# Another order of the seven products, and other places for their results, in a fused convolution and feed-forward kernel

## The chip, the cores and the metric

The kernel runs on one core of a Trainium2 chip. The metric is device time in microseconds (us), the median of several executions of one program; lower is better.

## The reference

`x` is 2048 rows of 1024. It is normalised by rows; `xn` goes into two branches whose results are added to `x`.

```python
xn = _layernorm(x)                         # x = A_q, 2048 x 1024
# A: gated convolution
k_shift = short causal convolution of k with shift_k (4 taps, per channel)
kv  = k_shift * v
y   = long causal convolution of kv with ssm_k (2048 taps, per channel) + kv * ssm_D
A   = xn * y
# B: feed-forward
h   = silu(xn @ w1)                        # w1: 1024 x 3584
B   = h @ w2                               # w2: 3584 x 1024
out = x + A + B
```

## The kernel before

**Products.** All matmuls take float16 operands, each split into a high and a low part, so one product of two blocks is three matmuls per chunk of 128 (lines L946 to L948 for `xn @ w1`, called GEMM1; L1074 to L1076 for `h @ w2`, called GEMM2).

**Seven in place of eight.** Most of GEMM1 and a part of GEMM2 multiply 2 x 2 blocks by seven products of sums and differences, named P1 to P7 (`PRODUCTS`, L50). `x` is held as seven sums (A11, A12, A22, S1 to S4), the weights likewise (B11, B21, B22, T1 to T4). One such group of products is a *unit*: in GEMM1 a pair of weight column blocks `i` for one half `sp` of the rows (12 units in the first half, 14 in the second, `UNITS`), in GEMM2 a quarter of the row tiles of one half (8 units, `tiles2`, `units2`). A product in a unit is twelve matmuls of 512 columns.

**Banks.** The products of a unit share PSUM banks of the ring `ff` (four banks). Bank `one` takes P1, then P2 on top. Bank `two` begins as a copy of P1 made by ScalarE (`ff<-ff` in the trace); P6 is added to it; ScalarE copies the sum out (called `u` in GEMM1, `a` in GEMM2); P5 is added; ScalarE copies it again (`d`); P3 is added. Bank `c` takes P7; VectorE forms c + d; P4 is added; VectorE forms c + u. Before, the order on TensorE is P1, then P7, P6, P2, P5, the next unit's P1, P3, P4. `units` and `units2` issue the products, `evacuate` and `evacuate2` empty the banks. A `Token` in `seen` stands for "copied out, the bank may be added to", one in `made` for "product done".

**Places in SBUF.** `places` are eight places of 1 MB: they hold the seven sums of `x`, later the converted blocks of `w2` (`W2PLACE` and `FPLACE` say which place, in the order in which the products leave them). The sums of the second half of the rows are brought by transposing loads on SyncE's queue (`load_x`, line L342), each as soon as its place is left by the first half. Place 4 holds A21 at first and then the *quads*: the results of the pairs of blocks 8 to 11 (`PAIRS`), which GEMM2 will use in seven products too (`quad`, `room`).

**Results** go through `hfs`, three tiles of two halves each (`hf` in the trace; `vs_r` and `ws_r` are the same object), and a second such object `hts` with two tiles (`ht`). A half is chosen by this rule, where `two` are the tiles of which both halves are free:

```python
k, h = min(self.free(), key=lambda q: (q[0] in two, self.age[q[0]]))
```

In `evacuate2` results leave as accumulating stores to `out`, issued by GpSimd (`G`, line L346). The very last block is instead loaded, added to and stored by SyncE's queue (`L`, line L336), to end sooner.

**GEMM2's plain part** takes the rows in two passes over the columns (`h`), in five chunks `c` of `w2`. `TOGETHER` says which row tiles are done at once: the first two in the first pass and the last three in the second share a chunk before the next is taken.

**The convolution** is a chain of transforms in eight groups of 128 channels beside all this: matmuls at L1520 to L1522 (forward) and L1711 to L1713 (back), much VectorE work (line L349, `spec` and `tmp`). `spare` lets it use a bank of `ff` in GEMM2's plain part if more than one is free.

**Order.** All instructions are put in an order at build time by a planner (`Order.run`): each generator is a stream; the planner takes the stream whose next instruction could begin first by its own estimates, less a small bias. A place or bank counts as free in the planner as soon as the last instruction that uses it has been put in order. On the chip each engine runs its instructions in that order and waits at semaphores.

Of the kernel before, what the change touches and what calls it, by code (L numbers as in the profile page):

```python
# [11 lines left out]
F32 = mybir.dt.float32  # L12
# [8 lines left out]
P = 128  # L21
# [4 lines left out]
NT = S // P  # L26
# [274 lines left out]
def h3_ffn_kernel(ctx, tc, x, kp, vs, fs, shift, dskip, w1, w2, cfwd, cinv, out):  # L301
# [559 lines left out]
    def room():  # L861

        for sp in range(2):
            yield flag["room", sp]
            yield places[4].ready
            t, tok = places[4].tile([P, 2, 2 * W], F32)
            parts.open(t, 2)
            yield flag["quads", sp]
            tok.set()
# [36 lines left out]
            add(blocks(i, b, hf, tok, (made,)), EB)  # L906
        return hf, made

    def evacuate(i, b, one, c, made, seen):
# [29 lines left out]
        add(silu(i, low, low, None, done), EB)  # L939

    def steps(o, w, xf, first, last, more=False):

# [39 lines left out]
    def units():  # L982

        todo = [(i, sp) for sp in range(2) for i in UNITS[sp]]
        yield ff.ready
        one = ff.tile([P, 4, P])
        yield from product("P1", *todo[0], one[0], True)
        for n, (i, sp) in enumerate(todo):
            if sp == 1:
                flag["unit", n - len(UNITS[0])].set()  # L990
                flag["room", 1].set()
            if i in PAIRS:
                add(quad(i, sp), 0.1)
            made, seen = defaultdict(Token), defaultdict(Token)
            yield ff.ready
            c = ff.tile([P, 4, P])
            add(evacuate(i, 2 * sp, one, c, made, seen), EB)
            yield from product("P7", i, sp, c[0], True)
            yield seen["P1"]
            two = seen["bank"][0]  # L1000
            yield from product("P6", i, sp, two)
            made["P6"].set()
            yield from product("P2", i, sp, one[0])
            made["P2"].set()
            yield seen["P6"]
            yield from product("P5", i, sp, two)
            made["P5"].set()
            if n + 1 < len(todo):
                yield ff.ready
                one = ff.tile([P, 4, P])  # L1010
# [5 lines left out]
            yield from product("P4", i, sp, c[0])  # L1016
# [14 lines left out]
    def feed_forward():  # L1031
# [13 lines left out]
        for h in range(2):  # L1045
            for ts in TOGETHER[h]:
# [34 lines left out]
    def uses2():  # L1081

        yield 0, "P1"
        for u in range(len(tiles2)):
            for n in ("P7", "P6", "P2", "P5"):
                yield u, n
            if u + 1 < len(tiles2):
                yield u + 1, "P1"
            yield u, "P3"
            yield u, "P4"  # L1090

    def units2():
# [8 lines left out]
            if u == len(tiles2) - 1:  # L1101
                wtok.set()

        yield ff.ready
        one = ff.tile([P, W])
        yield from product2("P1", 0, one[0], True)
        for u in range(len(tiles2)):
            made, seen = defaultdict(Token), defaultdict(Token)
            yield ff.ready
            c = ff.tile([P, W])  # L1110
            add(evacuate2(u, one, c, made, seen), EB)
            yield from product2("P7", u, c[0], True)
# [4 lines left out]
            yield from product2("P2", u, one[0])  # L1117
            made["P2"].set()
            yield seen["P6"]
            yield from product2("P5", u, two)  # L1120
            made["P5"].set()
            if u + 1 < len(tiles2):
                yield ff.ready
                one = ff.tile([P, W])
                yield from product2("P1", u + 1, one[0], True)
# [4 lines left out]
            yield from product2("P4", u, c[0])  # L1130
            made["P4"].set()

    def at(u, r, h):
# [2 lines left out]
        t = 4 * (2 * sp + r) + q  # L1136
        return orr[t // T2, t % T2, :, h * W:(h + 1) * W]

    def evacuate2(u, one, c, made, seen):
# [28 lines left out]
        seen["P7"].set()  # L1168
        yield G(at(u, 1, 1), d)
# [684 lines left out]
```

## Time and profile before

| what | us |
|---|---|
| median of 3 runs | 1257.39 (1256.72 to 1257.83) |
| the profiled execution | 1258.14 |
| its span, first to last instruction | 1256.4 |
| TensorE busy | 1232.6 (98%) |
| VectorE busy | 1117.9 (89%) |
| ScalarE busy | 790.5 (63%) |
| GpSimd busy | 83.5 (7%) |
| mean granted TensorE clock | 0.994 |

In the profile PE is TensorE, DVE VectorE, ACT ScalarE, POOL GpSimd, SP SyncE (SPq: what its queue issues). A row of the timeline has the start from the span's begin, the duration, engine and line, the operation with the tiles it writes and reads, the shapes, and in brackets the idle time before it and what ended that. A helper's line stands for all its calls: L349 two-operand VectorE operations, L352 the same with a scalar, L360 all ScalarE activations.

### The profile page before, as it was taken

To read this page: it belongs to the slowest core of one execution; us is meant where nothing else is said; L and a number is where in the kernel's file an instruction comes from. 1 tells how busy PE (TensorE), PEld (TensorE's weight loads), DVE (VectorE), ACT (ScalarE), POOL (GpSimd) and SP (SyncE) were. 2 spreads that over 40 slices of the span, in tenths; PEclk is the share of its full clock that TensorE was granted. 3 is DMA by queue.
4 is the path that set the end of the run, shared out by engine and by line. 5 is a ranking of instruction groups with operands and counts; after the bars stand their busy time and mean duration, and the time that the engine had idled before them with its cause. 6 is when DMAs were issued, how large, how long until landed. Compare 5 with 4: busy or idle time off the path is not lost. (4 is left out here: it accounts for less than half of the span.)

```text
span 1256.4 us, 17146 instructions
## 1 busy us (share of the span) xinstructions
PE 1232.6 (98%) x6034; PEld 597.5 (48%) x6034; DVE 1117.9 (89%) x1359; ACT 790.5 (63%) x1431; POOL 83.5 (7%) x93
## 2 busy tenths in 40 slices
PE   7999999999999999999999999999999999999996
PEld 6554444444444544444444544544544544454452
DVE  7999987997999789998999899799989889988970
ACT  7868888886588878568654643744653545563351
POOL 0000000000000000000000000000120030123132
PEclk8999999999999999999999999999999999999999
DMA  9276989989799899769984655688595497969765
GB/s 367 82 262 239 315 288 303 300 240 227 232 336 270 242 309 313 207 191 297 311 278 125 206 179 132 185 269 231 107 257 153 106 225 217 243 137 161 164 121 80
DMA packets 272662, 279.83 MB, mean 223 GB/s; under 512 B 73792, under 2 KB 192576, under 8 KB 271296
## 3 DMA queue, kind: packets, MB, share of 16 engines
q1 hardware_dynamic: 256848, 262.22, 67.9%
q0 software_dynamic: 15728, 16.52, 9.9%
q8 instruction: 47, 0.77, 0.3%
q14 instruction: 39, 0.32, 0.1%
HBM read 175.66 MB, written 88.34 MB: 210 GB/s over the span
## 5 line engine op out<-in xcount | busy, mean ns | idle before, releaser
L1074 PE MATMUL ff<-x,wo 128*128 128x512 f16 x864 | 327.9, 380 | 3.4 <-ACT hf L360 3.4
L1076 PE MATMUL ff<-x,wo 128*128 128x512 f16 x864 | 328.1, 380 | 0.0
L1075 PE MATMUL ff<-x,wo 128*128 128x512 f16 x864 | 327.9, 380 | 0.1
L946 PE MATMUL ff<-x,wo 128*128 128x512 f16 (+1 forms) x808 | 304.5, 377 | 6.2 <-ACT hf L360 3.0
L948 PE MATMUL ff<-x,wo 128*128 128x512 f16 (+1 forms) x808 | 304.8, 377 | 1.0 <-DVE wo L352 1.0
L947 PE MATMUL ff<-x,wo 128*128 128x512 f16 (+1 forms) x808 | 304.8, 377 | 0.0
L349 DVE TENSOR_TENSOR spec<-spec 128x512 f32<-128x512 f32 (+2 forms) x256 | 261.8, 1053 | 2.0
L1075 PEld LDWEIGHTS <-wo 128*128 128x128 f16 x864 | 84.6, 98 | 104.0 <-issue 4.7
L1076 PEld LDWEIGHTS <-wo 128*128 128x128 f16 x864 | 84.6, 98 | 102.6 <-issue 1.0
L1074 PEld LDWEIGHTS <-wo 128*128 128x128 f16 x864 | 85.5, 99 | 100.1 <-issue 0.6
L948 PEld LDWEIGHTS <-wo 128*128 128x128 f16 x808 | 79.6, 98 | 94.3 <-DVE wo L352 1.5
L947 PEld LDWEIGHTS <-wo 128*128 128x128 f16 x808 | 79.5, 98 | 93.8 <-issue 5.8
L946 PEld LDWEIGHTS <-wo 128*128 128x128 f16 x808 | 81.0, 100 | 90.2 <-ACT wo L360 1.7
L349 DVE TENSOR_TENSOR tmp<-spec 128x2048 f32<-128x2048 f32 (+1 forms) x48 | 92.7, 1933 | 0.9
L352 DVE SCALAR_TENSOR_TENSOR ht<-hf,wsc,ht 128x1024 f16<-128x1024 f32 (+1 forms) x56 | 67.4, 1203 | 7.5 <-ACT ht L360 7.2
L360 ACT ACTIVATE spec<-ps 128x512 f32<-128x512 f32 x92 | 53.2, 592 | 28.7 <-PE ps L1522 28.0
L352 DVE SCALAR_TENSOR_TENSOR wo<-raw,wsc,wo 128x512 f16<-128x512 f32 (+1 forms) x56 | 56.4, 1012 | 11.9 <-ACT wo L360 11.9
L346 POOL DMA_DIRECT2D out<-hf x47 | 45.8, 981 | 303.9 <-ACT hf L360 254.4
L360 ACT ACTIVATE hf<-ff,invc 128x512 f32<-128x512 f32 x32 | 21.9, 684 | 65.7 <-PE ff L1076 47.6
L360 ACT ACTIVATE ht<-hf,wsc 128x1024 f16<-128x1024 f32 (+1 forms) x56 | 60.8, 1085 | 3.4 <-DVE hf L349 2.1
L360 ACT ACTIVATE spec<-spec 128x1024 bf16<-128x1024 f32 x32 | 33.7, 1054 | 46.1 <-DVE spec L349 46.0
L349 DVE TENSOR_TENSOR spec<-tmp 128x512 f32<-128x512 f32 (+1 forms) x80 | 61.3, 792 | 0.7
(188 smaller groups left out, 1779.3 us busy)
## 6 DMA issues: line engine op xcount, KB each, us to landing
wo<-hs SPq DMA_DIRECT2D x160, 256.0 KB, 3.2
hs<-ht SPq DMA_DIRECT2D x80, 256.0 KB, 4.8
raw<-in_w SPq DMA_DIRECT2D x28, 512.0 KB, 5.9
wraw<-in_w SPq DMA_DIRECT2D x24, 512.0 KB, 5.4
w2n<-in_w SPq DMA_DIRECT2D x24, 512.0 KB, 6.1
out<-hf POOLq DMA_DIRECT2D x47, 256.0 KB, 4.5
kin<-in_kp SPq DMA_DIRECT2D x16, 704.0 KB, 5.1
xt<-in_x SPq DMA_DIRECT2D x16, 512.0 KB, 7.3
```

What stands on the lines that cost most here:

```text
L346: return Op("POOL", 1.1, 3.0, lambda: nc.gpsimd.dma_start(o, i, accum_op=ADD), [i], [o], m, 2.3 * n)
L349: return V(lambda: nc.vector.tensor_tensor(o, a, b, op=op), o, [a, b], **k)
L352: return V(lambda: nc.vector.scalar_tensor_tensor(o, a, s, b, op0=op0, op1=op1), o, [a, b] + ([] if isinstance(s, float) else [s]), **k)
L360: nc.scalar.activation(o, i, func, scale=scale, **kw)
L946: nc.tensor.matmul(o, w[:, 0, k], xf[:, :, k, 0], start=first and k == 0, stop=False, **kw)
L947: nc.tensor.matmul(o, w[:, 0, k], xf[:, :, k, 1], start=False, stop=False, **kw)
L948: nc.tensor.matmul(o, w[:, 1, k], xf[:, :, k, 0], start=False, stop=last and k == KH - 1, **kw)
L1074: nc.tensor.matmul(po, hx[:, n, 0, :], wc[:, n, 0, :], start=first and n == 0, stop=False, **kw)
L1075: nc.tensor.matmul(po, hx[:, n, 0, :], wc[:, n, 1, :], start=False, stop=False, **kw)
L1076: nc.tensor.matmul(po, hx[:, n, 1, :], wc[:, n, 0, :], start=False, stop=last and n == 3, **kw)
```

## The change

From the second unit on, in each of the two `units` functions, the order becomes P6, P7, P5, P2, next P1, P3, P4; the first unit keeps the old order. The emptying of a unit is started right after its P1 instead of after the unit before. The second half's S2 is loaded first, into place 4 (where the first half's quads were), and the second half's quads go to S2's old place 6; the other sums are loaded in the new order of use; `W2PLACE` and `FPLACE` follow. In GEMM2's first pass three row tiles share the chunks at the beginning instead of two. In the last unit the results of P1 with P2 and of P3, and the block that is loaded from `out`, may take a half of `hts` if none of `hfs` is free.

```diff
-W2PLACE = [(2, 7, 6, 3, 4), (0, 1, 5, 2, 7)]
-FPLACE = (6, 3, 4, 0, 1, 5, 2, 7)
+W2PLACE = [(2, 4, 7, 0, 3), (1, 5, 6, 2, 4)]
+FPLACE = (7, 0, 3, 1, 5, 6, 2, 4)
...
         for sp in range(2):
             yield flag["room", sp]
-            yield places[4].ready
-            t, tok = places[4].tile([P, 2, 2 * W], F32)
+            r = places[(4, XPLACE["S2"])[sp]]
+            yield r.ready
+            t, tok = r.tile([P, 2, 2 * W], F32)
...
-        yield made["P2"]
-        up, both = yield from places_of(i, b)
-        add(silu(i, up[:, 0], *one, both), EB)
+
+        def first():
+            up, both = quads_up[i, b] = yield from places_of(i, b)
+            add(silu(i, up[:, 0], *one, both), EB)
+        if early:
+            yield made["P2"]
+            yield from first()
         yield ws_r.ready
         d, dt = ws_r.tile([P, 4, P])
         yield made["P5"]
         yield a_act(d, two, AF.Copy)
         seen["P5"].set()
+        c = seen["c"]
+        if not early:
+            yield made["P2"]
+            yield from first()
+        up, both = quads_up.pop((i, b))
...
+        def start(n):
+            i, sp = todo[n]
+            yield ff.ready
+            one = ff.tile([P, 4, P])
+            yield from product("P1", i, sp, one[0], True)
+            made, seen = defaultdict(Token), defaultdict(Token)
+            add(evacuate(i, 2 * sp, one, made, seen, n == 0), EB)
+            return one, made, seen
...
+            if n == 0:
+                yield from seventh()
             yield seen["P1"]
             two = seen["bank"][0]
             yield from product("P6", i, sp, two)
             made["P6"].set()
-            yield from product("P2", i, sp, one[0])
-            made["P2"].set()
+            yield from second() if n == 0 else seventh()
             yield seen["P6"]
             yield from product("P5", i, sp, two)
             made["P5"].set()
+            if n > 0:
+                yield from second()
             if n + 1 < len(todo):
-                yield ff.ready
-                one = ff.tile([P, 4, P])
-                yield from product("P1", *todo[n + 1], one[0], True)
+                following = yield from start(n + 1)
...
-        for name in [p[0] for p in PRODUCTS.values()]:
-            r = places[XPLACE[name]]
+        for name in ("S2", "A11", "S3", "S1", "A12", "S4", "A22"):
+            r = places[4 if name == "S2" else XPLACE[name]]
...
-    TOGETHER = ([range(2)] + [(t,) for t in range(2, NT)],
+    TOGETHER = ([range(3)] + [(t,) for t in range(3, NT)],
...
-            for n in ("P7", "P6", "P2", "P5"):
+            for n in ("P7", "P6", "P2", "P5") if u == 0 else ("P6", "P7", "P5", "P2"):
...
         def copied(src, tok, to):
-            yield hfs.ready
-            o, otok = hfs.tile([P, W])
+            yield lambda: hfs.ready() or last and hts.ready()
+            o, otok = (hfs if hfs.ready() else hts).tile([P, W])
...
-        yield made["P2"]
-        add(copied(*one, at(u, 0, 0)), EB)
+        if u == 0:
+            yield made["P2"]
+            add(copied(*one, at(u, 0, 0)), EB)
         yield ws_r.ready
         d, dt = ws_r.tile([P, W])
         yield made["P5"]
         yield a_act(d, two, AF.Copy, invc2[:, 0:1])
         seen["P5"].set()
+        c = seen["c"]
         yield v_stt(d, c[0], invc2[:, 0:1], d, MUL, ADD)
         seen["P7"].set()
+        if u > 0:
+            yield made["P2"]
+            add(copied(*one, at(u, 0, 0)), EB)
         yield G(at(u, 1, 1), d)
         dt.set()
         if last:
             yield flag["conv out"]
-            yield hfs.ready
-            o, otok = hfs.tile([P, W])
+            yield lambda: hfs.ready() or hts.ready()
+            o, otok = (hfs if hfs.ready() else hts).tile([P, W])
```

`units2` is changed as `units` is, with its own `start`, `seventh` and `second`.

More of the change, by code (lines that the diff above doesn't have):

```diff
@@ L907, in places_of, with evacuate @@
         return hf, made
-    def evacuate(i, b, one, c, made, seen):
+    def evacuate(i, b, one, made, seen, early):
         yield ff.ready
@@ L939, in evacuate @@
         add(silu(i, low, low, None, done), EB)
+    quads_up = {}
     def steps(o, w, xf, first, last, more=False):
@@ L984, in units @@
         todo = [(i, sp) for sp in range(2) for i in UNITS[sp]]
-        yield ff.ready
-        one = ff.tile([P, 4, P])
-        yield from product("P1", *todo[0], one[0], True)
+        def start(n):
[6 more added lines that the diff above has]
+            return one, made, seen
+        following = yield from start(0)
         for n, (i, sp) in enumerate(todo):
@@ L993, in units, with seventh, second @@
                 add(quad(i, sp), 0.1)
[L994 to L998, printed above, removed]
+            one, made, seen = following
+            def seventh():
+                yield ff.ready
+                seen["c"] = c = ff.tile([P, 4, P])
+                yield from product("P7", i, sp, c[0], True)
+            def second():
+                yield from product("P2", i, sp, one[0])
+                made["P2"].set()
+            if n == 0:
+                yield from seventh()
             yield seen["P1"]
@@ L1015, in units @@
             yield seen["P7"]
-            yield from product("P4", i, sp, c[0])
+            yield from product("P4", i, sp, seen["c"][0])
             made["P4"].set()
@@ L1102, in product2, with start, seventh, second @@
                 wtok.set()
-        yield ff.ready
-        one = ff.tile([P, W])
-        yield from product2("P1", 0, one[0], True)
-        for u in range(len(tiles2)):
[L1108 to L1112, printed above, removed]
+        def start(u):
+            yield ff.ready
+            one = ff.tile([P, W])
+            yield from product2("P1", u, one[0], True)
+            made, seen = defaultdict(Token), defaultdict(Token)
+            add(evacuate2(u, one, made, seen), EB)
+            return one, made, seen
+        following = yield from start(0)
+        for u in range(len(tiles2)):
+            one, made, seen = following
+            def seventh():
+                yield ff.ready
+                seen["c"] = c = ff.tile([P, W])
+                yield from product2("P7", u, c[0], True)
+            def second():
+                yield from product2("P2", u, one[0])
+                made["P2"].set()
+            if u == 0:
+                yield from seventh()
             yield seen["P1"]
@@ L1116, in units2 @@
             made["P6"].set()
-            yield from product2("P2", u, one[0])
-            made["P2"].set()
+            yield from second() if u == 0 else seventh()
             yield seen["P6"]
@@ L1121, in units2 @@
             made["P5"].set()
+            if u > 0:
+                yield from second()
             if u + 1 < len(tiles2):
-                yield ff.ready
-                one = ff.tile([P, W])
-                yield from product2("P1", u + 1, one[0], True)
+                following = yield from start(u + 1)
             yield seen["P5"]
@@ L1129, in units2 @@
             yield seen["P7"]
-            yield from product2("P4", u, c[0])
+            yield from product2("P4", u, seen["c"][0])
             made["P4"].set()
```

6 lines of the change are left out of this document (3 added, 3 removed).

## The prediction

> **What bounds the kernel now.** I read the page first: how busy each engine is.
>
> ```profile
> PE 1232.6 (98%) x6034; PEld 597.5 (48%) x6034; DVE 1117.9 (89%) x1359; ACT 790.5 (63%) x1431; POOL 83.5 (7%) x93
> ```
>
> TensorE works in 1232.6 of 1256.4 us, and the change takes no matmul away. All that can be won is idle time, the clock that idle time costs, and what follows the last matmul. So the second view is the table of stretches (columns: stretch, length, busy time of PE, PEld, DVE, ACT, POOL, granted clock, DMA share, GB/s).
>
> ```profile
> 320.00:330.00 10.00, 8.24 (x39) 3.63 (x38) 9.96 (x9) 6.66 (x9) 0.76 (x1) 1.00 0.37 125
> 584.00:598.00 14.00, 11.04 (x44) 4.64 (x43) 11.85 (x13) 11.37 (x20) 0.00 (x0) 0.88 1.09 360
> 598.00:1077.00 479.00, 478.41 (x2325) 227.46 (x2323) 445.66 (x478) 247.26 (x505) 33.92 (x35) 1.00 0.71 199
> 1231.00:1257.00 26.00, 14.91 (x61) 6.09 (x59) 2.19 (x3) 2.75 (x4) 4.53 (x6) 0.87 0.48 76
> ```
>
> Three places lose time: 1.76 us in the first, 2.96 in the second with a clock of 0.88, and 11.1 in the last. The 479 us of plain GEMM2 lose 0.6. Third, the timeline of those places. The last unit of GEMM1, on PE and then on ACT:
>
> ```profile
> 584.66 0.38 PE L948 MATMUL ff<-x,wo 128*128 128x512 f16 x1
> 588.00 0.40 PE L946 MATMUL ff<-x,wo 128*128 128x512 f16 x1 [2.96 <-ACT hf L360]
> 588.22 0.61 PE L947 MATMUL ff<-x,wo 128*128 128x512 f16 x1
> ...
> 591.61 0.40 PE L1520 MATMUL ps<-hi,cfw 128*128 128x512 f16 x1
> ```
>
> ```profile
> 583.97 1.15 ACT L360 ACTIVATE x<-w2n,tau 128x1024 f16<-128x1024 f32 x1 [1.19 <-DMA w2n<-in_w]
> ...
> 587.37 0.58 ACT L360 ACTIVATE hf<-ff 128x512 f32<-128x512 f32 x1
> ```
>
> P5 ends at 585.04 (584.66 + 0.38); P3 adds into the same bank and may start only when ACT has copied it, and that copy, behind other work of ACT's, ends at 587.95. This last unit has no next P1 to put between them. The first unit of the second half waits for DVE instead:
>
> ```profile
> 318.72 4.61 DVE L349 TENSOR_TENSOR spec<-spec 128x2048 f32<-128x2048 f32 x2
> ...
> 325.63 0.69 DVE L349 TENSOR_TENSOR hf<-ff,hf 128x512 f32<-128x512 f32 x1
> ```
>
> ```profile
> 321.64 0.38 PE L948 MATMUL ff<-x,wo 128*128 128x512 f16 x1
> ...
> 324.23 0.38 PE L948 MATMUL ff<-x,wo 128*128 128x512 f16 x1
> 326.37 0.38 PE L946 MATMUL ff<-x,wo 128*128 128x512 f16 x1 [1.76 <-DVE hf L349]
> ```
>
> The first two PE rows are the last matmuls of P1 and of P3: twelve starts in 2.59 us, so a product takes 2.59 and a matmul 0.216. P4 (326.37) needs the sum c + d (325.63), which stood behind 7 us of other DVE work. At the end of the kernel, POOL (accumulating stores), then ACT, SP and DVE:
>
> ```profile
> 1224.26 1.43 POOL L346 DMA_DIRECT2D out<-hf  x1
> 1224.85 1.94 POOL L346 DMA_DIRECT2D out<-ht  x1
> 1230.07 1.11 POOL L346 DMA_DIRECT2D out<-ht  x1 [3.27 <-issue]
> 1234.09 1.77 POOL L346 DMA_DIRECT2D out<-hf  x2 [2.91 <-issue]
> 1241.48 0.86 POOL L346 DMA_DIRECT2D out<-hf  x1 [5.63 <-ACT hf L360]
> 1245.16 0.86 POOL L346 DMA_DIRECT2D out<-hf  x1 [2.81 <-DVE hf L352]
> 1250.61 0.86 POOL L346 DMA_DIRECT2D out<-hf  x1 [4.60 <-ACT hf L360]
> ```
>
> ```profile
> 1240.44 0.69 ACT L360 ACTIVATE hf<-ff,invc 128x512 f32<-128x512 f32 x1 [1.47 <-DMA out<-hf]
> 1243.27 0.69 ACT L360 ACTIVATE hf<-ff,invc 128x512 f32<-128x512 f32 x1 [2.13 <-PE ff L1076]
> 1249.62 0.69 ACT L360 ACTIVATE hf<-ff,invc 128x512 f32<-128x512 f32 x1 [5.67 <-DVE hf L349]
> ```
>
> ```profile
> 1245.45 0.33 SPq L336 DMA_DIRECT2D hf<-out  x1
> ```
>
> ```profile
> 1221.86 0.69 DVE L349 TENSOR_TENSOR ht<-py,ht 128x512 f32<-128x512 f32 x1 [1.05 <-ACT py L360]
> 1222.46 0.75 DVE L352 SCALAR_TENSOR_TENSOR hf<-ff,invc,hf 128x512 f32<-128x512 f32 x1
> 1228.64 0.75 DVE L352 SCALAR_TENSOR_TENSOR hf<-ff,invc,hf 128x512 f32<-128x512 f32 x1 [5.42 <-PE ff L1076]
> 1243.98 0.75 DVE L352 SCALAR_TENSOR_TENSOR hf<-ff,invc,hf 128x512 f32<-128x512 f32 x1 [14.60 <-ACT hf L360]
> 1248.84 0.69 DVE L349 TENSOR_TENSOR hf<-hf 128x512 f32<-128x512 f32 x1 [4.11 <-DMA hf<-out]
> ```
>
> POOL's rows are, in order: unit 6's sum from P5; two of the convolution's; unit 6's copy of P3 and its last sum; then unit 7's copy of P2, its sum from P5, its copy of P3. ACT's three are unit 7's copies of P2, P5 and P3. Read it backwards. The last store (1250.61) follows a copy (1249.62) that waited for the place left by the add (1248.84); the add waited for the load (1245.45), the load for the place of the store at 1241.48, that store for its copy (1240.44), that copy for the place of the second store at 1234.09. Those two waited behind the convolution's last store (1230.07), which touches the rows of the one at 1224.26 and began only 5.8 us after it. So the end is a chain of places and stores; PE's waits there only follow it. The code says why the six halves of hf don't help: a half whose other half is held is taken first, so the newest places are used again and the idle ones are not.
>
> **The change part by part.**
>
> *New order in units, middle.* P5 to P3 now has P2 and, but for the last unit, P1 between them. For the unit at 325 the distance from P5's end to P4 grows by one product, 2.59; the sum was late by 1.9 (326.37 less 324.45, one step behind P3's last start). That wait goes: -1.9. For the last GEMM1 unit, P5's copy took 2.9 us and P2 covers 2.59, which leaves 0.3 to 0.5. The wait is 588.00 less 584.66 less 0.22, or 3.1. Behind it eight matmuls (588.22 to 591.61) took 3.39 where 8 x 0.216 is 1.73: 1.7 more. A remaining wait of 0.5 leaves the clock alone, since 1.76 did at 326. So -3.1 - 1.7 + 0.5 = -4.3, together -6.2. The Trainium skill (TensorE: Matmul & The Clock Gate, section "Why this matters for your kernels") puts the limit at gaps of about 3 us; here 2.96 already halved the pace, so by the page the 1.7 would not belong to this wait and the sum would be -4.5; the measured pace stands.
>
> *What the order tightens.* From P1 to P6 there were P3, P4 and P7; now P3 and P4, 5.18 us, for the copy of P1's bank. Before:
>
> ```profile
> 327.25 0.58 ACT L360 ACTIVATE ff<-ff 128x512 f32<-128x512 f32 x1
> ```
>
> P1 ended at 322.0 (321.64 + 0.38), its copy at 327.8, 5.8 later, where the new P6 would start after 5.2: 0.6 too late. But the copy was not begun earlier because its generator was started only after P4; the change starts it right after P1. The bank it needs is that of the unit before, free one activation behind P2 (0.69 for this shape in the ACT rows above), while P1 runs. Price between 0 and 0.6 per unit; I take 0, the nearer reason. P6 to P5 has one product between, as before.
>
> *S2 first.* The second half's factors come by seven transposing loads, each of which holds SP. The first of them, A11, before, and how long they take to land:
>
> ```profile
> 273.69 4.72 SPq L342 DMA_TRANSPOSE x<-xspA  x1
> ```
>
> ```profile
> DMA to landing us min/median/max: 5.0/6.9/9.2
> ```
>
> ```profile
> 291.64 0.38 PE L946 MATMUL ff<-x,wo 128*128 128x512 f16 x1
> ```
>
> S2 goes ahead of A11 on SP and must wait until the quads have left its place. With one load of 4.72 ahead, A11 would be issued at 278.4 and land by 287.6 at the latest (9.2). P1 of the second half starts at 291.64 (the fifth product of the half's last unit, counted in twelves). If the quads leave later, each us beyond 4 is a us of waiting on PE, 4.7 at the most if I let one whole load show. So 0 to 4.7; I take 0. What stands behind these loads on SP (two hs and two raw loads) keeps as much SP time ahead of it as before.
>
> *Three row tiles, remapped places.* PE lost 0.6 us between 598 and 1077, so -0.6 to 0; the remapping follows the order in which products release their places. A third bank in use leaves the convolution no spare one for 13 us more (five chunks of 2.59); PE has GEMM2 work to do meanwhile. I take 0.
>
> *More places at the end.* The second ring is asked only if no half of hf is free; the last unit holds five of six at most (copies of P6, P2, P5 and P3, and the load), so by the code it is hardly used: 0, down to what rival 1 gives.
>
> *New order at the end.* P5's copy, sum and store now go ahead of P2's on ACT and POOL; P2's have P3 and P4 to hide beside, 5.2 us. On before's clock unit 7 starts at 1228.4 (the DVE row at 1228.64 follows P4). P6, P7, P5 end 7.8 later, at 1236.2; the copy (0.69) lets the DVE step start at 1237.0; store 1.18 later (1243.98 to 1245.16), 1238.2; its place, now the one the load takes, is free 3.97 later (1241.48 to 1245.45), 1242.2; add 3.39 later, 1245.6; from add to the end of the span 7.56: 1253.1 for 1256.4, -3.3. With the middle's -6.2 that is -9.5, if the place of P5's copy is free, and P3 and P4 end in time beside it (1236.2 + 7.8 = 1244.0, before the add). It is the place of unit 6's last store, which hangs on the convolution. DVE was busy 9.96 of 10 us around 325 and hardly waited for PE, so the convolution need not come earlier: its last product ends at 1222.55, store from 1223.0, the next stores 4.02 later (1230.07 to 1234.09), 1227.0, the second one's place 6.35 later (1234.09 to 1240.44), 1233.4. Without that wait P5's copy would start at 1236.2 - 6.2 = 1230.0. So 3.3 of the 9.5 are lost: -6.2. If that store comes 2.5 later, behind those around 1224: -3.7. I take -6.2, since it uses only when the data is ready.
>
> The profiled execution took 1258.14, span 1256.4; the median is 1257.39. The sum is a difference, so 1258.14 becomes 1251.9 and the median 1251.2.
>
> **The rivals.**
> 1. *The end opens wholly*: the load gets an idle place, the convolution follows PE. Then the last store hangs on the place free at 1242.2: copy, 0.99 to its store (1249.62 to 1250.61), 5.8 to the end: 1249.0, -7.4, with -6.2 the time is 1243.8. For: idle halves exist. Against: the way places are chosen. 0.12.
> 2. *P6 waits for P1's copy*, on the slower side: 32 units use the new order, so 0.6 each is 19 us, 1270.4. From 0.27 each (8.7 over 32) the kernel is slower than now by 2.5. For: the row at 327.25, and ACT has the second-half's and the convolution's copies to do beside (790.5 us in all). Against: the copy is started earlier. 0.20, of which a quarter stays near no change.
> 3. *The last GEMM1 unit waits on*: ACT is again held by a w2 load (1.19 at 583.97) and P2 doesn't cover it: 4.3 less, 1255.5. 0.14.
>
> **How the numbers follow.** The forecast has 0.54: 1251.2, by itself 1247.9 (-9.5) to 1253.7 (-3.7). About 0.2%, 2.5 us, is what a measurement can tell from no change. Faster: 0.54 + 0.12 + half of rival 3 (0.07) = 0.73; same: 0.07 + 0.05 = 0.12; slower: 0.15. The range runs from 1244.0, at rival 1, to 1261.0, rival 2 at 0.31 each; above it lies about 0.12, below about 0.06.
>
> **What would show it.** Right: no idle of 2.96 on PE at the end of GEMM1 and clock 1.00 there; no wait for the sum near 325; the first accumulating store of unit 7 from P5, not from P2; the load of out some 9 us earlier. Wrong: waits of matmuls for ff<-ff copies, a wait at the half's start for x, or the load of out still landing last behind a store at the same distance from the end.

## The result, and the profile after

The kernel after takes 1257.40 us (median; 1255.07 to 1260.69), the kernel before 1256.64 beside it: ratio 1.0007, 95% interval 0.9998 to 1.0016. No change was measured where 6.2 us less was forecast. The profiled execution took 1257.22 us with a span of 1255.0. Busy time, and the table of stretches (same columns as in the prediction, its four stretches on the new clock):

```profile
PE 1232.0 (98%) x6034; PEld 597.0 (48%) x6034; DVE 1116.1 (89%) x1359; ACT 788.1 (63%) x1431; POOL 83.4 (7%) x93
```

```profile
317.00:327.00 10.00, 9.85 (x47) 4.39 (x45) 9.96 (x11) 4.19 (x6) 0.76 (x1) 1.00 0.81 270
580.00:594.00 14.00, 14.00 (x66) 6.37 (x65) 12.73 (x15) 13.34 (x20) 0.00 (x0) 1.00 1.01 312
594.00:1077.00 483.00, 479.42 (x2319) 227.32 (x2317) 446.96 (x478) 244.59 (x501) 32.21 (x33) 1.00 0.73 202
1230.00:1256.00 26.00, 15.97 (x74) 7.05 (x72) 2.95 (x4) 2.75 (x4) 4.35 (x5) 0.91 0.47 74
```

Two of the three losing places are gone: PE fills the first stretch but for 0.15 us and the second wholly, at a clock of 1.00. The third row is new: GEMM2, which lost 0.6 us, now loses 3.6. GEMM2's first matmul, before and then after:

```profile
597.46 0.38 PE L1074 MATMUL ff<-x,wo 128*128 128x512 f16 x1
```

```profile
593.84 0.38 PE L1100 MATMUL ff<-x,wo 128*128 128x512 f16 x1
```

It comes 3.6 us earlier. But 1.3 of that was there before anything that the change touches: TensorE's order is the same in both for the first 536 matmuls, and one of its rows from these (before, then after) is already early, because the granted clock rose later in the execution of the kernel before (0.84 over the first 22 us, against 0.92):

```profile
22.60 1.47 PE L598 MATMUL ft<-ident,xt 128*128 128x128 f32 x12
```

```profile
21.27 1.47 PE L598 MATMUL ft<-ident,xt 128*128 128x128 f32 x12
```

So GEMM1's part of the change is worth 2.3 us here, where 6.2 were forecast. Six of the convolution's matmuls (1.3 us) also moved ahead of GEMM2's first. Most of the rest went to new waits between the two mended places (before, then after; TensorE lost nothing there before and loses 1.9 us now):

```profile
340.00:584.00 244.00, 244.00 (x1186) 116.00 (x1185) 227.25 (x263) 189.43 (x338) 0.76 (x1) 1.00 0.88 268
```

```profile
340.00:584.00 244.00, 242.14 (x1173) 114.69 (x1172) 225.53 (x264) 192.86 (x349) 1.51 (x2) 1.00 0.88 270
```

The last unit's start comes no earlier: the DVE row of unit 6's last sum, at 1228.64 before, now reads 1230.47 (DVE, SP and POOL at the end):

```profile
1230.47 0.75 DVE L352 SCALAR_TENSOR_TENSOR hf<-ff,invc,hf 128x512 f32<-128x512 f32 x1 [8.02 <-PE ff L1102]
...
1247.89 0.69 DVE L349 TENSOR_TENSOR hf<-hf 128x512 f32<-128x512 f32 x1 [8.18 <-DMA hf<-out]
```

```profile
1244.33 0.34 SPq L336 DMA_DIRECT2D hf<-out  x1
```

```profile
1232.03 1.77 POOL L346 DMA_DIRECT2D out<-hf  x2 [3.17 <-issue]
1240.13 0.86 POOL L346 DMA_DIRECT2D out<-hf  x1 [6.33 <-DVE hf L352]
1241.82 0.86 POOL L346 DMA_DIRECT2D out<-hf  x1 [0.83 <-ACT hf L360]
1249.71 0.86 POOL L346 DMA_DIRECT2D out<-hf  x1 [7.03 <-ACT hf L360]
```

So the account of the span is: -3.62 to the start of GEMM2 (-1.33 by the clock at the start, -2.29 behind it), +5.45 from there to unit 6's last sum (1230.47 - 593.84 against 1228.64 - 597.46), -3.23 from there to the end (1255.0 - 1230.47 against 1256.4 - 1228.64): -1.4 in all, in one execution each. The end does what was forecast: unit 7's first store is P5's (1240.13), and the load of out takes its place (1244.33). What was won in GEMM1 was lost in GEMM2. The waits of PE in that part (waiter, releaser, us in total, times, longest), before first:

```profile
PE ps L1520 <- ACT tmp L360: 0.6, 1, 0.6
```

```profile
PE ps L1563 <- ACT tmp L360: 3.8, 4, 2.3
PE ff L1100 <- ACT hf L360: 0.9, 1, 0.9
```

The waiting matmuls are the convolution's forward transforms (L1563, ps). The longest wait in the timeline of PE:

```profile
680.85 0.38 PE L1102 MATMUL ff<-x,wo 128*128 128x512 f16 x1
683.55 0.38 PE L1563 MATMUL ps<-hi,cfw 128*128 128x512 f16 x1 [2.33 <-ACT tmp L360]
...
684.93 0.63 PE L1563 MATMUL ff<-hi,cfw 128*128 128x512 f16 x1
685.36 0.63 PE L1564 MATMUL ff<-lo,cfw 128*128 128x512 f16 x1
...
688.48 0.38 PE L1563 MATMUL ps<-hi,cfw 128*128 128x512 f16 x1
```

ps is ready for the next sum only when ACT has copied the last one into tmp, and that copy waits until the group before has given its part of the spectrum free: a chain over DVE and ACT. From 684.9 to 688.1 starts stand 0.43 apart, twice 0.215, so the wait cost its 2.33 us and about 1.6 us of pace in this execution. The waits of 4.7 us and this pace, less the 0.6 us that the kernel before waits, make 5.7 us, about the 5.45 of the account.

### The profile page after: what moved, and what is told of

The parts are those of the page before. It is cut to its first block, busy times and chain, and to the rows that moved or that the text cites. A ratio compares the mean times of both kernels' runs of the same rounds, so it can differ in the third digit from the quotient of the medians.

```text
span 1255.0 us, 17166 instructions
## 1 busy us (share of the span) xinstructions
PE 1232.0 (98%) x6034; PEld 597.0 (48%) x6034; DVE 1116.1 (89%) x1359; ACT 788.1 (63%) x1431; POOL 83.4 (7%) x93
## 4 chain that ended last, share of the span: by engine, by line
PE 67%; DVE 18%; DMA 6%; issue 5%; ACT 2%; POOL 1%; SPq 1%; POOLq 0%; DVEq 0%; ACTq 0%
PE ff L958 11%; PE ff L960 11%; PE ff L959 11%; PE ff L1100 9%; PE ff L1102 9%; PE ff L1101 9%; DVE spec L349 7%; DVE tmp L349 3%; PE ps L1563 2%; DVE spec L352 2%; PE ps L1565 2%; PE ps L1564 2%; DVE x L352 1%; DVE acc L352 1%; DMA wraw<-in_w 1%
## 5 line engine op out<-in xcount | busy, mean ns | idle before, releaser
L352 DVE SCALAR_TENSOR_TENSOR acc<-kin,taps,acc 128x1024 f32<-128x1024 f32 x48 | 61.5, 1281 | 4.7 <-ACT acc L360 4.6
```

The source lines that it names most:

```text
L352: return V(lambda: nc.vector.scalar_tensor_tensor(o, a, s, b, op0=op0, op1=op1), o, [a, b] + ([] if isinstance(s, float) else [s]), **k)
```

## The experiments

**Theory 1**: after GEMM1, TensorE's order is fixed and threads the convolution's matmuls between those of GEMM2; a lead of TensorE that the convolution's chain does not share is given back there. **Theory 2**: TensorE is bound by its own work, and the waits belong to the new order as such, or to chance. **Theory 3**: GEMM1's own new waits ate the gain. Ratios are to the kernel before, timed beside each; about nine in ten single executions lie within 2.5 us of their kernel's median, the farthest 5.6 us off.

| kernel | median us | ratio (95%) |
|---|---|---|
| after | 1257.40 | 1.0007 (0.9998 to 1.0016) |
| after_dve_less | 1252.33 | 0.9959 (0.9944 to 0.9974) |
| before_dve_less | 1255.53 | 0.9996 (0.9984 to 1.0007) |
| after_pe_plus | 1256.34 | 1.0000 (0.9987 to 1.0012) |
| before_pe_plus | 1258.24 | 1.0016 (1.0005 to 1.0028) |
| end_order | 1253.64 | 0.9978 (0.9970 to 0.9987) |
| gemm1_order | 1259.73 | 1.0021 (1.0012 to 1.0031) |
| after_plan_pe | 1257.88 | 1.0008 (0.9996 to 1.0021) |
| after_late_conv | 1257.74 | 1.0006 (0.9996 to 1.0016) |
| after_s2_late | 1255.64 | 0.9995 (0.9985 to 1.0005) |
| end_s2_first | 1253.50 | 0.9975 (0.9966 to 0.9985) |
| after_last_unit | 1252.73 | 0.9976 (0.9966 to 0.9986) |
| after_replan | 1254.04 | 0.9984 (0.9972 to 0.9996) |
| before_replan | 1253.71 | 0.9976 (0.9967 to 0.9986) |
| after_idle_places | 1252.90 | 0.9965 (0.9953 to 0.9977) |
| end_idle_places | 1250.07 | 0.9954 (0.9938 to 0.9969) |
| last_unit_idle | 1249.39 | 0.9947 (0.9934 to 0.9960) |
| replan_idle | 1247.53 | 0.9927 (0.9913 to 0.9940) |
| last_unit_idle_replan | 1247.18 | 0.9930 (0.9918 to 0.9943) |

**Less work for the convolution's chain.**

```diff
 o = steps_of(tmp, P, (2 * P, 8))
-yield v_tt(o, o, run(k, 0, 8), ADD)
+q = steps_of(tmp, P, (2 * P, 2)), run(k, 0, 2)
+yield V(lambda q=q: nc.vector.tensor_tensor(q[0], q[0], q[1], op=ADD), o, [o, run(k, 0, 8)])
```

> The kernel after with less VectorE work in the convolution: of the addition that finishes the four products of each frequency block (the result tmp read and written in place, 32 instructions of 1.225 us) only a quarter of the width is computed, so part of the convolution's result is left out; the planner's costs, and with them the order of every engine, are unchanged. That takes about 0.88 us off each of 32 VectorE instructions, 28 us in all, some 20 of them after GEMM1. Theory 1 (after GEMM1 TensorE keeps running into the convolution, whose chain over VectorE and ScalarE is late for the place that the fixed order gives its matmuls, and that is where the microseconds won earlier went): the waits of the convolution's matmuls in GEMM2, 7.1 us now, fall to under 1 us, and the time falls by 5 to 8 us against the kernel before, to about 1250. Theory 2 (TensorE is simply bound by its own work and by the waits for copies of GEMM1's new order): the time falls by less than 2 us, to 1255 to 1258, since the copies are ScalarE's.

> The same quarter-width addition in the kernel before (part of the convolution's result is left out, order unchanged). Theory 1: its convolution matmuls wait only 1.05 us in GEMM2, so it gains 1 to 2 us there, plus what the wait of 1.9 us at 326 us gives: -1 to -3 us, and the kernel after with the same cut is then 4 to 6 us faster than this one. Theory 2: both gain the same, within 1 us of one another.

(The 7.1 us in these texts are in no view: the views have 3.8 us for the waits of those matmuls, 4.7 us idle in all, and about 1.6 us of pace behind the longest.) The kernel after gained 0.48% (6.0 us), the kernel before 0.04%, within its interval. Against the kernel before that is 0.41% (5.2 us), the low end of theory 1's 5 to 8; the kernel before gained less than its 1 to 3. PE in GEMM2 of the kernel after, and of this one (stretch, length, busy PE):

```profile
594.00:1215.00 621.00, 616.33 (x2989) 292.93 (x2987) 570.26 (x614) 308.75 (x617) 64.59 (x69) 1.00 0.75 193
```

```profile
597.00:1215.00 618.00, 617.85 (x3018) 295.43 (x3017) 551.29 (x615) 310.67 (x618) 68.60 (x72) 1.00 0.75 194
```

The idle time fell from 4.67 to 0.15 us. A part of that is TensorE's, which comes to GEMM2 2.7 us later in this execution; the time says that the chain's work mattered. Theory 2 as bound by TensorE's own work is out. But the two kernels stand 0.37% (4.6 us) apart, of which the end explains 3.2; GEMM1's gain is hardly to be seen even here, where GEMM1 waits 4.3 us in three places for ACT copies in the profiled execution, so theory 3 holds a part.

**More work for TensorE.**

```diff
 def mm(n=n):
+    for _ in range(idle_work.pop() if idle_work and first and n == 0 else 0):   # 14, once
+        nc.tensor.matmul(po, hx[:, n, 0, :], wc[:, n, 0, :], start=True, stop=True)
```

> The kernel after with 14 more matmuls of 128x512 (0.216 us each, 3.0 us in all) at the start of GEMM2, whose sums the unit's first matmul overwrites; order otherwise unchanged. Theory 1: TensorE then comes 3 us later to the convolution, whose waits in GEMM2 shrink by about 3 us, so the time is within 1 us of the kernel after. Theory 2: TensorE is the bound, and the time grows by the whole 3.0 us.

> The same 14 matmuls, 3.0 us, at the start of GEMM2 of the kernel before. Theory 1: its convolution matmuls wait only 1.05 us there, so only about 1 us is absorbed and the time grows by 2 to 3 us. Theory 2: it grows by 3.0 us, as the kernel after does.

Three us of matmuls cost the kernel after nothing (-0.07%, not told from none) and the kernel before 0.16% (2.0 us). PE in GEMM2 of after_pe_plus, idle 0.5 us now:

```profile
594.00:1215.00 621.00, 620.49 (x3025) 296.01 (x3023) 571.15 (x616) 311.18 (x619) 67.14 (x71) 1.00 0.76 193
```

Order and instructions are otherwise the same, so no new plan is in play. This agrees with theory 1: at GEMM2's start the kernel after has 3 us to give away, the kernel before about 1 (its interval, 0.6 to 3.5 us of cost, also holds theory 2's 3.0; the kernel after decides).

**The parts alone.** end_order is the kernel before with the hunks of units2 and evacuate2; gemm1_order the kernel before with all others but TOGETHER. Both begin GEMM2 with two row tiles, though the text of end_order says three; so do end_s2_first, end_idle_places and replan_idle below.

> The kernel before with GEMM2's part of the change alone: the new order of the units, three row tiles to begin and more places at the end; GEMM1 is the old one. Theory 1 (microseconds won before the convolution are given back at its matmuls, those won behind its last matmul stay): the 3.3 us of the end stay, and TensorE comes to GEMM2 as late as before, so the convolution's matmuls wait about 1 to 2 us there: -2 to -3.5 us, 1253 to 1254.5. Theory 2 (the waits in GEMM2 come with its new order and not with an earlier TensorE): the same 5 to 7 us of waits as in the kernel after, and 0 to +3 us.

> The kernel before with GEMM1's part of the change alone (new order of its units, S2 first to the quads' place); GEMM2 begins with two row tiles and runs and ends as before. Theory 1: GEMM1 ends 2 to 4 us earlier and the waits of the convolution's matmuls in GEMM2 grow by about as much; the end's 3.3 us are not won: 1256 to 1258, no change. Theory 2 (GEMM1's 2.3 us stay if GEMM2 keeps its old order): 1253.5 to 1255.

end_order keeps 0.22% (2.8 us), and PE has no wait at all in its GEMM2:

```profile
594.00:1215.00 621.00, 621.00 (x3034) 297.14 (x3033) 572.57 (x618) 316.49 (x628) 68.21 (x72) 1.00 0.73 193
```

TensorE's order here is that of the kernel before up to 1109 us, since GEMM2's units come last: the run shows that the end's gain stays, and the new order of those units can't be what makes a wait at 683 us. GEMM1's part makes things worse, with it (1.0007 against 0.9978) and alone (1.0021), more than theory 1 said. Waits of PE in gemm1_order's GEMM2:

```profile
PE ff L1101 <- DVE x L352: 3.4, 2, 2.6
PE ff L1100 <- DMA wo<-hsfS: 1.5, 1, 1.5
PE ff L1100 <- ACT hf L360: 1.0, 1, 1.0
PE ps L1546 <- ACT tmp L360: 0.9, 1, 0.9
```

Here TensorE, early again, runs mainly into w2's factors (DVE x, at 616 to 622 us) which are still being made while the first row tiles run, not into the convolution. The kernel after has the same order up to GEMM2 and differs there, until long after 683 us, only in its three row tiles: it has no wait at 616 to 622, and waits at 683.55 instead. So the lead is given back at whichever chain comes first, and the number of row tiles bears on which. No run has three row tiles by themselves.

**Moving the waiting matmuls.** Two edits of the planner's figures, both on the kernel after:

```diff
-            yield T(mm, po, [hx[:, n], wc[:, n]], 3 * 0.2185)                # after_plan_pe
+            yield T(mm, po, [hx[:, n], wc[:, n]], 3 * 0.2160)
-                            yield T(mm, ps, [hi, lo], 0.65, m=1.0)           # after_late_conv
+                            yield T(mm, ps, [hi, lo], 0.65, m=2.0 if g == 3 else 1.0)
```

> The kernel after, where the planner counts 0.648 us for three matmuls of GEMM2 in place of 0.6555 (the trace has 0.2155 us from one to the next): no instruction is added or removed, but the planner lets TensorE do more of GEMM2 before each group of the convolution's matmuls. Theory 1: their waits, 7.1 us in GEMM2, fall to 1 to 3 us, and the time falls by 3 to 5 us against the kernel after, to 1252 to 1254. Theory 2: TensorE's waits stay as many in other places, and the time is within 1.5 us of the kernel after.

> The kernel after with one constant: for the fourth group of the convolution the planner keeps its forward matmuls 2 us, in place of 1, behind their data. The order of TensorE is that of the kernel after up to the wait at 680.85 us; there, 3 matmuls of GEMM2 (0.65 us) and 6 of the inverse transform (about 0.65 us) now run ahead of the waiting ones. Theory 1: that wait, 2.49 us, becomes about 1.2 us and no longer halves the pace behind it (1.3 us), 2.6 us gained there, if the order that follows brings no new waits: 1254 to 1256. Theory 2 (any order of these pays as much somewhere): within 1 us of the kernel after, 1256 to 1258.

Neither gained, as theory 2 had forecast for both; theory 1's gains of 3 to 5 and of 2.6 us did not come. In after_plan_pe the convolution's matmuls wait no more, but w2's factors are late at 1091 to 1097 us:

```profile
PE ff L1101 <- DVE x L352: 2.3, 2, 1.3
PE ff L1100 <- ACT x L360: 1.4, 2, 0.8
```

Its profiled execution (1253.09) is its fastest, so these rows do not show what its median of 1257.88 pays. In after_late_conv the inverse transform's matmuls, moved ahead of the waiting ones, need the same chain, and the wait only changed hands:

```profile
682.33 0.38 PE L1102 MATMUL ff<-x,wo 128*128 128x512 f16 x1
682.86 0.27 PE L1754 MATMUL py<-zh,civ 128*128 128x256 f16 x1 [0.15 <-ACT zh L360]
685.14 0.27 PE L1755 MATMUL py<-zl,civ 128*128 128x256 f16 x1 [2.01 <-DVE zl L352]
```

My figure for it, 2.6 us, was wrong: what ran ahead was not free work.

**Which part of GEMM1.**

```diff
-            add(evacuate(i, 2 * sp, one, made, seen, n == 0), EB)            # after_last_unit
+            add(evacuate(i, 2 * sp, one, made, seen, n < len(todo) - 1), EB)
...                                                                           # n == 0, n > 0 likewise
-        for name in ("S2", "A11", "S3", "S1", "A12", "S4", "A22"):           # after_s2_late
+        for name in ("A11", "S2", "S3", "S1", "A12", "S4", "A22"):
...
```

after_s2_late also puts S2 and the quads back to their old places and exchanges places 4 and 6 in the lists for w2's factors; end_s2_first is end_order with S2 first and the new places.

> The kernel after, but in GEMM1 only the very last unit runs in the new order; the others keep P7, P6, P2, P5. So the waits for ScalarE's copies between P6 and P5 (0.91, 0.25, 0.65 us and smaller in the kernel after) should go, and both won places stay (the sum at 326, the last unit). Theory 1 (what GEMM1 wins is given back at the convolution's matmuls in GEMM2): GEMM1 ends at 590 to 592.5, 1 to 3 us earlier than in the kernel after, and the wait at about 680 grows to 4 to 6 us; the time is no better than that of the kernel with GEMM2's part alone (1253.6), 1254 to 1257. Theory 3 (it was the waits inside GEMM1 that ate the gain): the time falls to 1250 to 1252, since the two gains then add to the end's 3.3 us.

> The kernel after with the second half's S2 loaded second and to its old place, and the places of the w2 factors as before. Theory 1: where P1's first operand comes later, GEMM1's second half begins about 1.9 us later (the wait at 323 us is back), and the wait at 680 us shrinks by as much: within 1 us of the kernel after, 1256 to 1258.5, or a little faster. Theory 3: the 1.9 us are lost at the end: 1259.

> GEMM2's part of the change and S2 first, with the old order of GEMM1's units. Theory 1: TensorE comes up to 2 us earlier to the convolution than with GEMM2's part alone (1253.6), and waits there as much longer; 1253 to 1256. Theory 3: the 1.9 us stay, 1251.7.

The new order of the middle units costs 0.31% in this plan (1.0007 against 0.9976). What the last unit and S2 then win in GEMM1 adds nothing to end_order (0.9976 and 0.9975 against 0.9978), as theory 1 has it and theory 3 has not. But theory 1's road was another: it had a wait of 4 to 6 us near 680 in after_last_unit, where 0.85 is found, and in after_s2_late a wait shorter by 1.9 us, where it is 0.5; and end_s2_first gives its lead back to w2's factors, not to the convolution (waits of PE in its GEMM2):

```profile
PE ff L1076 <- DVE x L352: 3.7, 2, 2.1
```

In these plans the wait for the sum near 325 goes with S2, not with the order of the units; a new plan alone removes it too, for before_replan below has no wait between 300 and 340 us. Waits of PE from 300 to 340 us in after_s2_late (new order, old S2), and the stretch there in end_s2_first (old order, new S2):

```profile
PE ff L958 <- DVE hf L349: 2.2, 1, 2.2
```

```profile
318.00:328.00 10.00, 10.00 (x48) 4.54 (x47) 9.93 (x10) 3.92 (x6) 0.76 (x1) 1.00 0.69 223
```

**Chance.** The same work in a new plan:

```diff
-    EB = 0.06
+    EB = 0.07
```

> The kernel after, planned anew with the bias of the evacuating streams at 0.07 in place of 0.06: the same instructions in a somewhat different order. If the loss comes by TensorE's early arrival, it stays in any such order: within 1.5 us of the kernel after. If it is chance, the time moves by 2 to 4 us to either side.

> The kernel before with the same constant at 0.07: the size of the chance in an order of the kernel before. Within 1.5 us of the kernel before by theory 1; 2 to 4 us to either side if any new order moves the time as the change did.

Both gained 0.23 to 0.24% (3 us), inside the 2 to 4 us that chance was to give and outside theory 1's 1.5: a plan's chance is as large as the effect under study. In the new plans, too, the change as a whole brings nothing (0.9984 with it, 0.9976 without). Why does before_replan keep what it wins before GEMM2, which begins at 591.55 us there? The convolution comes along. First forward matmul of the convolution's fourth group on PE, and ACT's scale of its third group; after, then before_replan:

```profile
663.26 0.38 PE L1563 MATMUL ps<-hi,cfw 128*128 128x512 f16 x1
```

```profile
675.25 0.31 ACT L480 ACTIVATE csc<-rstd,csc 128x16 f32<-128x16 f32 x1
```

```profile
662.27 0.38 PE L1520 MATMUL ps<-hi,cfw 128*128 128x512 f16 x1
```

```profile
672.08 0.31 ACT L480 ACTIVATE csc<-rstd,csc 128x16 f32<-128x16 f32 x1
```

TensorE is as early in both; the chain is 3.2 us earlier in the second. The same two rows from twelve traces, with the idle time of the fourth group's transforms behind them:

| kernel | PE at | scale at | apart | PE then waits |
|---|---|---|---|---|
| after_dve_less | 665.99 | 674.05 | 8.06 | 0 |
| end_order | 665.56 | 674.99 | 9.43 | 0 |
| before | 668.17 | 677.61 | 9.44 | 0 |
| before_replan | 662.27 | 672.08 | 9.81 | 0 |
| after_pe_plus | 666.98 | 676.89 | 9.91 | 0.44 |
| after_plan_pe | 662.80 | 672.73 | 9.93 | 0 |
| after_last_unit | 667.61 | 677.94 | 10.33 | 0.85 |
| after_s2_late | 665.16 | 676.50 | 11.34 | 1.87 |
| after_replan | 664.32 | 675.90 | 11.58 | 1.44 |
| after | 663.26 | 675.25 | 11.99 | 2.33 |
| after_idle_places | 664.47 | 676.93 | 12.46 | 2.33 |
| after_late_conv | 663.40 | 676.07 | 12.67 | 0, and 2.16 in the inverse transform |

The eight other traces agree: six stand 6.92 to 9.44 us apart with no wait, last_unit_idle_replan 9.77 with 0.29 and last_unit_idle 10.31 with 0.83. Below 9.7 us apart TensorE doesn't wait, from there to 9.93 it waits 0 to 0.44, and beyond, but for after_late_conv, what is over 9.8 to within half a us. The rows of after, after_dve_less, after_pe_plus and after_idle_places have one and the same order of TensorE up to there, so the relation is not one of plans. Early or late on the clock decides nothing; the lead over the chain does. Theory 1 stands in this form; that TensorE's early arrival alone sets the wait does not.

Two limits: every kernel that waits here begins GEMM2 with three row tiles, which no run varies alone. And the table tells of this one wait, not of the time: gemm1_order does not wait here (9.35 us apart) and is the slowest.

**The end, with the idle places used.**

```diff
-            o, otok = (hfs if hfs.ready() else hts).tile([P, W])             # the last unit's copies
+            o, otok = (hts if last and hts.ready() else hfs).tile([P, W])
-            o, otok = (hfs if hfs.ready() else hts).tile([P, W])             # the load of out
+            o, otok = (hts if hts.ready() else hfs).tile([P, W])
```

> The kernel after, where the load of out and the last unit's copies take a place of the second ring (idle at the end) first, and a place of the first only when that has none: the load of out no longer waits for the store that holds its place (1244.3 us), and starts with the last unit. Both theories: the last add needs only the last sums, TensorE's last matmul at 1245.8 is unchanged, and from it to the end there is one addition, one store and its landing: 3 to 4.5 us less than the kernel after, 1252.5 to 1254. If the stores' queue sets the end instead, the gain is under 1 us.

> GEMM2's part of the change with GEMM1 as before, and the load of out and the last unit's copies to the second ring's places first. With the kernel after, the same edit took the end from about 9.0 us behind TensorE's last matmul to 5.3. All theories: 3 to 4.5 us less than GEMM2's part alone, 1249 to 1251, the fastest of all so far.

The kernel after gained 0.42% (5.3 us), end_order 0.24% (3.0). DVE at the end of after_idle_places, then the last accumulating store there:

```profile
1238.73 0.68 DVE L349 TENSOR_TENSOR hf<-hf,ht 128x512 f32<-128x512 f32 x1
1244.24 0.75 DVE L352 SCALAR_TENSOR_TENSOR hf<-ff,invc,hf 128x512 f32<-128x512 f32 x1 [4.83 <-PE ff L1102]
```

```profile
1242.69 0.86 POOL L346 DMA_DIRECT2D out<-ht  x1 [1.71 <-ACT ht L360]
```

The add runs at 1238.73, not at 1247.89, and the last sum follows PE's last matmul: the end hangs on TensorE again. The versions that join the parts that paid:

> The kernel after with the old order of GEMM1's units but for the last one (1252.7 us) and with the second ring's places first for the load of out and the last unit's copies (which took 3.5 to 4.5 us from two kernels): 1248 to 1249.5, the fastest so far. If the two overlap at the end: 1250 to 1252.

> GEMM2's part of the change with the idle places first and GEMM1 as before (1250.1 us), planned anew with the constant at 0.07, as the kernel before was when it gained 2.4 us. There TensorE and the convolution both came 6 us earlier in the trace, and no wait took it back. If such a gain adds to the end's: 1247 to 1248.5, the ratio 0.9925 to 0.994. If it only took the place of the end's: 1250.

> The new order for GEMM1's last unit alone, S2 first, GEMM2's part and the idle places first (1249.4 us), planned anew with the constant at 0.07. The same two ways: 1246.5 to 1248.5 if the convolution comes earlier in this order as well, 1249 to 1251 if TensorE alone does and then waits for it.

All three add up about as expected: 0.53%, 0.73% and 0.70% less than the kernel before; the last two are the fastest, some 10 us below the kernel after.

## Why the prediction was wrong

- *New order in units, -1.9 near 325.* The wait fell to 0.15 us, but not by the order: with the new order and the old S2 it is 2.2, with the old order and the new S2 it is gone.
- *The last GEMM1 unit, -4.3.* Right: no wait, clock 1.00. Rival 3 did not come.
- *P6 behind P1's copy, 0.* Right: no wait for an ff<-ff copy shows, and rival 2 did not come. But the sentence that P6 to P5 stays as it was missed that ACT's copy of P6 came later, and it was priced at nothing. The new waits of PE for such copies up to 594 us in the kernel after, 1.2 us in two (with smaller ones and two of the convolution's, PE loses 1.9 us there):

```profile
PE ff L958 <- ACT hf L360: 1.2, 2, 0.7
```

- *S2 first, 0.* No loss on its own load showed; it brought the wait at 325 to nothing, and the total stays within the intervals (1.0007 with it, 0.9995 without).
- *Three tiles, -0.6 to 0.* Their effect alone was not run. gemm1_order, with two, waits 3.4 us for w2's factors; the kernel after, with three, does not, and waits for the convolution instead. That "PE has GEMM2 work to do meanwhile" did not hold at 683.55 us.
- *Places at the end, 0.* Right: hardly used as written; asked first, they are worth 3 to 5 us, by rival 1's mechanism.
- *New order at the end, -3.3 on its own clock.* Right: -3.23, and end_order keeps it. The 3.3 us that the sum then gave up again to the convolution's last stores were not put to the test, since TensorE came to unit 7 no earlier; for the same reason the load of out came 1.1 us earlier and not 9.
- *The step that failed* is the one that carried the middle's -6.2 to the end. First, the -6.2 itself: behind the start's 1.33 us, GEMM2 begins only 2.3 us earlier, since the new order's own waits in GEMM1 were priced at 0. Second, the sum has no term for what TensorE meets in GEMM2. "PE lost 0.6 us between 598 and 1077" says only that PE and the convolution's chain were in step; the table has the kernel before at 9.44 us, some 0.4 short of waiting. I used the sentence that the convolution "need not come earlier" for the last stores alone, and not for the five groups of transforms that TensorE runs within GEMM2 before them. The earlier start was followed by +5.45: what was won was given back, with the halved pace behind a wait on top in this execution.

Open stays why the chain's third group comes late in the kernel after, and what part the three row tiles have in it. The experiments vary it mostly through new plans, and these move the time by 3 us with no change in the work.

## What to carry to other kernels

Time saved on the busiest engine reaches the end only if what its fixed order meets later comes earlier too: for each later meeting with a second chain, read how far apart the two pass by now and count only that slack. An engine that shows no wait in a stage is not thereby free to start it sooner. And where a planner makes the order, plan the same work anew once or twice first: here that alone moved the time by 0.24%, as much as the part of the change that paid.

## What the hardware showed beyond that

Whether an idle time halves TensorE's pace is not told by its length. 2.33 us did in the kernel after (from 684.9, for 3.2 us) and did not in after_idle_places, at the same matmul (685.25); nor did 2.88 us at GEMM1's end in end_order (587.08), where 2.96 did in the kernel before. What tells is where the idle time lies. In each of the twenty traces the granted clock changes only at times that stand whole multiples of 3.41 us apart, and where this grid lies differs from execution to execution. Two stretches of the grid around each of the four waits (columns as in the prediction's table: length, busy PE first, granted clock third from the end), in the kernel after, after_idle_places, the kernel before and end_order:

```profile
681.34:684.75 3.41, 1.20 (x6) 0.58 (x6) 3.41 (x4) 3.00 (x5) 0.00 (x0) 1.00 0.32 77
684.75:688.16 3.41, 3.41 (x15) 1.85 (x13) 2.67 (x4) 2.05 (x4) 0.00 (x0) 0.50 0.33 67
```

```profile
681.08:684.50 3.42, 1.84 (x9) 0.73 (x8) 3.42 (x4) 1.98 (x2) 0.00 (x0) 1.00 0.37 95
684.50:687.91 3.41, 2.67 (x16) 1.53 (x16) 3.25 (x4) 2.95 (x7) 0.00 (x0) 1.00 0.15 58
```

```profile
584.81:588.22 3.41, 0.45 (x4) 0.10 (x2) 2.77 (x5) 3.31 (x8) 0.00 (x0) 1.00 1.15 343
588.22:591.64 3.42, 3.42 (x10) 1.22 (x9) 3.39 (x4) 1.86 (x6) 0.00 (x0) 0.50 1.06 325
```

```profile
582.31:585.72 3.41, 1.89 (x9) 0.78 (x8) 3.09 (x4) 2.58 (x5) 0.00 (x0) 1.00 1.01 299
585.72:589.14 3.42, 2.06 (x10) 0.97 (x10) 3.07 (x5) 3.42 (x9) 0.00 (x0) 1.00 1.15 338
```

In the first and the third, 2.21 and 2.96 us of idle time lie in one stretch, and the next runs at half the clock; in the two others the grid cuts the wait into 1.58 and 0.74, and into 1.52 and 1.36, and the clock stays. From 25 us on, in all twenty traces, a stretch at full clock in which PE idled 2.13 us or more (the least: end_idle_places, from 583.87) was followed by one at half clock, and one in which it idled 2.07 or less (the most: before_dve_less, from 1235.22) was not. So the 1.7 us of pace in the prediction's term for the last unit were partly chance: end_order has the same order and nearly the same wait without them. The Trainium skill (TensorE: Matmul & The Clock Gate, section "Why this matters for your kernels") advises against gaps of more than about 3 us; here gaps of 2.33 to 2.96 us went both ways, by where they lay.
